# A retention layer and a squared-ReLU FFN on one core: additions moved from GpSimd to VectorE, outer sums made in phase one, inner products interleaved

## The chip, the cores and the metric

The kernel runs on one core of a Trainium2 chip. The metric is device time in microseconds (us), the median of several runs. The profile is one execution of the program taken by the hardware profiler; TensorE, VectorE, ScalarE, GpSimd and SyncE stand in it as PE, DVE, ACT, POOL and SP, and PEld is TensorE's weight load.

## The reference

Inputs are float32 except `w_in` and `w_out`, which arrive as 64-bit floats and are rounded to float32 in the kernel.

```python
# q, k, v: (8, 8, 576, 64)
scores = scale * np.matmul(q, k.transpose(0, 1, 3, 2))
Dmat = np.where(rel >= 0, gamma[:, None, None] ** rel[None, :, :], 0.0)
attn_out = np.matmul(scores * Dmat[None, :, :, :], v)
x = attn_out.transpose(0, 2, 1, 3).reshape(4608, 512)
h = np.maximum(x @ w_in, 0.0)          # w_in: 512 x 2048
out = h * h @ w_out                    # w_out: 2048 x 512
```

## The kernel before

**Phase one** walks over 40 chunks of attention (five to each of eight batches: four of 128 tokens, one of 64). A chunk i goes through `turn` (transposes of q and k), `scores` and `retain`, one stage to an iteration, and its result lands transposed in `xT`. When 512 tokens are there they make a block (nine in all), and the block's first FFN product is cut into 28 steps, four groups (`mp`) of seven, which `ffn` deals out between the attention's stages by tokens. The schedule is manual: each engine takes its instructions in the order in which the code records them.

Both FFN products are made with Strassen's scheme in Winograd's form, seven products instead of eight (`PRODUCTS`). The left operands are the four quarters A11, A12, A21, A22 and sums S1 to S4, the right ones B quarters and T1 to T4. Products add up in three PSUM tiles a, b and c, so a product that adds to a tile waits until the copy of what the tile held so far has been taken. In phase one a product is `h_a`, `h_b` or `h_c`: four float32 matmuls of 256 columns, each of which TensorE runs as two passes. `ffn_in` takes the results out of PSUM, adds them, squares them and leaves the quarters g11, g12, g21, g22 of the FFN's hidden layer in SBUF; `keep_g` stores the four of a group in DRAM (`g_dram`).

**Weights.** `w_in` comes in 16 pieces and `w_out` in 16, each rounded by `round_a` and `round_b`: integer work on VectorE, three passes on ScalarE, two multiplications on GpSimd. `sum_w_in` makes the four weight sums of a piece pair on GpSimd. `prepare` does one piece at a time, every second step of block 0 and later every seventh step; the `w_out` pieces and their sums go to `w2_dram`.

**Phase two** makes the second FFN product, block by block, with Strassen twice: seven outer products `ffn_out(n, j)`, each of seven inner products of four float32 matmuls of 128 columns (`o_a`, `o_b`, `o_c`, eight passes each; 63 times 7 = 441 inner products in all). The outer sums S1 to S4 of a block's quarters are made here by `outer_sum` over 128x2048 elements (S1 and S3 on GpSimd, S2 and S4 on VectorE), the inner sums of the next outer product by `inner_sums` over 128x512 (two on VectorE, two on GpSimd) after the fourth inner product. An outer product's inner products run in the order `INNER`, and its results p1, u2, p15 and r are 128x128 additions. At its end one or two 128x512 additions put r into the output quarters c11 to c22.

SyncE issues all loads and stores on one queue, in the order of the code.

Of the kernel before, what the change touches and what calls it, by code (L numbers as in the profile page):

```python
# [36 lines left out]
INNER = (1, 0, 2, 4, 3, 5, 6)  # L37
# [3 lines left out]
def kernel(  # L41
# [10 lines left out]
):  # L52

# [57 lines left out]
    g_dram = dram.tile([N_BLK, 4, 128, N_M, HT], F32, name="g_dram")  # L111
    room = [const.tile([128, N_M * HT], F32, name=f"room{j}") for j in range(7)]
# [68 lines left out]
    def round_a(j):  # L181
        lo, hi, frac, sign = words_of(j)
        exp = exp_of(j).bitcast(U32)
        t = piece_dst(j).bitcast(U32)
        nc.vector.tensor_scalar(exp, hi, 20, 0x7FF, op0=ALU.logical_shift_right, op1=ALU.bitwise_and)

        nc.vector.tensor_scalar(t, as_dst(j, hi), 0xFFFFF, 0x100000, op0=ALU.bitwise_and, op1=ALU.bitwise_or)

        nc.scalar.activation(frac, lo, AF.Copy, scale=2.0 ** -52)

        nc.scalar.activation(exp, exp, AF.Relu, bias=exp_bias[:, 0:1], scale=2.0 ** 23)

        nc.scalar.activation(sign, hi, AF.Sign, bias=exp_bias[:, 1:2], scale=-1.0)

    def round_b(j):
        lo, hi, frac, sign = words_of(j)
        t = piece_dst(j)
        nc.gpsimd.tensor_tensor(exp_of(j), exp_of(j), sign, op=ALU.mult)
        nc.vector.scalar_tensor_tensor(t, t.bitcast(U32), 2.0 ** -20, as_dst(j, frac), op0=ALU.mult, op1=ALU.add)  # L199
        nc.gpsimd.tensor_tensor(t, t, as_dst(j, exp_of(j)), op=ALU.mult)  # L200

    def sum_w_in(m):

        a11, a12, a21, a22, s1, s2, s4 = (w_in[m // 2][:, m % 2, j, :, :] for j in range(NP))
        nc.gpsimd.tensor_tensor(s1, a21, a22, op=ALU.add)
        nc.gpsimd.tensor_tensor(s2, s1, a11, op=ALU.subtract)
        nc.gpsimd.tensor_tensor(s4, a12, s2, op=ALU.subtract)
        nc.gpsimd.tensor_tensor(a21, a11, a21, op=ALU.subtract)

    def sum_w_out(m):  # L210

        mh = m // N_MQ
        b11, b12, b21, b22 = (stage[0][:, j, 2 * mh:2 * mh + 2, :] for j in range(4))
        t1, t2, t4 = (stage[1][:, j, 2 * mh:2 * mh + 2, :] for j in range(3))
        nc.vector.tensor_tensor(t1, b12, b11, op=ALU.subtract)
        nc.vector.tensor_tensor(b12, b22, b12, op=ALU.subtract)
        nc.vector.tensor_tensor(t2, b22, t1, op=ALU.subtract)
        nc.vector.tensor_tensor(t4, b21, t2, op=ALU.subtract)

    def keep_w_out(mq):  # L220

        for st_, at in ((stage[0], slice(0, 4)), (stage[1], slice(4, 7))):
            b11, b12, b21, b22, t1, t2, t4 = (st_[:, :, j, :] for j in range(NP))
            nc.vector.tensor_tensor(t1, b12, b11, op=ALU.subtract)
            nc.vector.tensor_tensor(b12, b22, b12, op=ALU.subtract)
            nc.vector.tensor_tensor(t2, b22, t1, op=ALU.subtract)
            nc.vector.tensor_tensor(t4, b21, t2, op=ALU.subtract)
            nc.sync.dma_start(w2_dram[at, :, mq, :].rearrange("o p f -> p o f"),
                              st_.rearrange("p o s f -> p o (s f)"))

    n_made = [0]

    def prepare():

        j = n_made[0]
        if j > len(pieces):
            return
        n_made[0] += 1

        for part in ((finish, begin) if j > N_W1 else (begin, finish)):  # L240
            part(j if part is begin else j - 1)
# [458 lines left out]
```

## Time and profile before

| | |
|---|---|
| median of 3 runs | 1276.17 us (1274.11 to 1276.55) |
| the profiled execution | 1276.56 us, its span 1274.9 us |
| TensorE busy, matmuls | 1087.6 us, 85% of the span |
| VectorE busy | 750.3 us, 59% |
| GpSimd busy | 467.3 us, 37% |
| ScalarE busy | 204.0 us, 16% |

The span runs from the first instruction to the last. Matmuls are pipelined and their ends are modelled, so a busy TensorE is not one at its full pace; how fast it goes is read from the distance between the starts of its groups. Clock 1.0 in a row means 2.4 GHz granted, 0.5 means 1.2 GHz.

### The profile page before, as it was taken

The numbers are of one execution on the slowest core, as the hardware profiler recorded it, in microseconds if no ns is written. First come the engines' busy times: TensorE is split into PE (matmuls) and PEld (weight loads), VectorE is DVE, ScalarE is ACT, GpSimd is POOL, SyncE is SP. The second block draws the span as 40 slices with busy tenths as digits, with TensorE's granted clock in tenths as the row PEclk, the third lists the DMA queues.
The fourth block names the chain that finished last, engine by engine and source line by source line (L and its number), as shares of the span: only waits on it lengthen the run. The fifth ranks groups of instructions, "written<-read, shape, count | busy, mean of one in ns | idle before, by whom it ended". The sixth has DMA issues, their size and how long they took to land. (4 is left out here: it accounts for less than half of the span.)

```text
span 1274.9 us, 19815 instructions
## 1 busy us (share of the span) xinstructions
PE 1087.6 (85%) x8168; PEld 981.9 (77%) x8168; DVE 750.3 (59%) x1108; ACT 204.0 (16%) x443; POOL 467.3 (37%) x346
## 2 busy tenths in 40 slices
PE   6389979989898999999999587787878788787788
PEld 5377868878687888887878487787877787787788
DVE  4588656656566444444444475757566656666755
ACT  4344212232231121111100000000000000000000
POOL 3888312323132121212110544434434444353532
PEclk9689989989899999999999797989889888888889
DMA  9834754664653644442177343131303030303000
GB/s 243 223 89 123 180 196 116 162 208 133 192 131 127 159 125 112 104 105 69 67 308 259 130 169 103 63 125 41 132 35 132 34 132 34 132 34 133 34 34 34
DMA packets 158362, 158.20 MB, mean 124 GB/s; under 512 B 114880, under 2 KB 124096, under 8 KB 152768
## 3 DMA queue, kind: packets, MB, share of 16 engines
q1 hardware_dynamic: 158272, 156.93, 40.8%
q8 instruction: 65, 1.06, 0.4%
q14 instruction: 25, 0.20, 0.1%
HBM read 96.88 MB, written 60.03 MB: 123 GB/s over the span
## 5 line engine op out<-in xcount | busy, mean ns | idle before, releaser
L406 PE MATMUL h_b<-room,w 128*128 128x256 f32 x864 | 223.9, 405 | 55.5 <-DVE room L425 33.6
L576 PE MATMUL o_b<-w,room 128*128 128x128 f32 x1176 | 172.9, 298 | 99.9 <-DVE small L581 99.9
L576 PEld LDWEIGHTS o_b<-w,room 128*128 128x128 f32 x1176 | 156.0, 209 | 107.5 <-issue 63.3
L406 PEld LDWEIGHTS h_b<-room,w 128*128 128x128 f32 x864 | 168.5, 201 | 85.8 <-DVE room L425 35.8
L576 PE MATMUL o_c<-w,room 128*128 128x128 f32 x1008 | 144.1, 290 | 0.0
L406 PE MATMUL h_a<-room,w 128*128 128x256 f32 x576 | 140.5, 388 | 0.0
L406 PE MATMUL h_c<-room,w 128*128 128x256 f32 x576 | 138.4, 383 | 0.0
L576 PEld LDWEIGHTS o_c<-w,room 128*128 128x128 f32 x1008 | 134.9, 208 | 0.0
L406 PEld LDWEIGHTS h_a<-room,w 128*128 128x128 f32 x576 | 109.9, 194 | 16.9
L423 POOL TENSOR_TENSOR room<-room 128x512 f32<-128x512 f32 x36 | 39.1, 1085 | 225.8 <-ACT room L422 220.6
L406 PEld LDWEIGHTS h_c<-room,w 128*128 128x128 f32 x576 | 107.4, 191 | 14.6
L326 POOL TENSOR_TENSOR vs<-v_ld,dv 128x512 f32<-128x512 f32 (+1 forms) x40 | 43.1, 1077 | 132.0 <-issue 61.2
L413 DVE SCALAR_TENSOR_TENSOR room<-room 128x512 f32<-128x512 f32 x108 | 86.8, 804 | 3.7
L418 DVE TENSOR_TENSOR room<-h_b,room 128x512 f32<-128x512 f32 x36 | 24.9, 692 | 108.3 <-PE h_b L406 108.0
L547 POOL TENSOR_TENSOR room<-a,room 128x512 f32<-128x512 f32 x24 | 30.6, 1273 | 127.3 <-PE o_c L576 50.8
L200 POOL TENSOR_TENSOR w<-w,w 128x512 f32<-128x512 f32 x32 | 42.0, 1314 | 84.1 <-DVE w L199 68.3
L425 DVE TENSOR_TENSOR room<-h_b,room 128x512 f32<-128x512 f32 x36 | 24.8, 689 | 72.5 <-PE h_b L406 72.5
L547 POOL TENSOR_TENSOR room<-room,room 128x512 f32<-128x512 f32 x21 | 26.6, 1268 | 100.5 <-PE o_c L576 65.4
L344 PE MATMUL x_ps<-ret,vs 128*64 128x128 f32 (+1 forms) x640 | 59.3, 276 | 4.2 <-POOL vs L326 4.2
L322 DVE TENSOR_TENSOR ret<-sc,msk 128x512 f32<-128x512 f32 (+1 forms) x80 | 47.1, 629 | 22.2 <-PE sc L317 22.2
L587 ACT COPY r<-o_a 128x128 f32<-128x128 f32 x54 | 14.3, 265 | 267.1 <-PE o_a L576 154.4
L576 PE MATMUL o_a<-w,a 128*128 128x128 f32 x384 | 55.5, 292 | 0.0
(101 smaller groups left out, 1739.6 us busy)
## 6 DMA issues: line engine op xcount, KB each, us to landing
g_dram<-room SPq DMA_DIRECT2D x36, 1024.0 KB, 4.9
a<-g_dram SPq DMA_DIRECT2D x24, 1024.0 KB, 5.5
w<-w_dram SPq DMA_DIRECT2D x7, 1792.0 KB, 9.0
room<-g_dram SPq DMA_DIRECT2D x12, 1024.0 KB, 5.6
out_dram<-room SPq DMA_DIRECT2D x18, 512.0 KB, 3.4
q_ld<-in_q_dram SPq DMA_DIRECT2D x32, 256.0 KB, 5.0
k_ld<-in_k_dram SPq DMA_DIRECT2D x32, 256.0 KB, 5.1
v_ld<-in_v_dram SPq DMA_DIRECT2D x32, 256.0 KB, 5.2
```

The lines of the kernel that those rows point to most:

```text
L200: nc.gpsimd.tensor_tensor(t, t, as_dst(j, exp_of(j)), op=ALU.mult)
L322: nc.vector.tensor_tensor(r[:cs, :, :cs], sc[e][:cs, :, :cs], msk[:cs, :, :cs].to_broadcast([cs, HP, cs]), op=ALU.mult)
L326: nc.gpsimd.tensor_tensor(vs[:cs], loaded[i][2][:cs], dv[:cs, :, ci:ci + 1].to_broadcast([cs, H, D]), op=ALU.mult)
L344: nc.tensor.matmul(p[half, hp, :cs], lhsT=s["vs"][:cs, 2 * hp + e, :], rhs=s["ret"][e][:cs, hp, :cs], start=(ci == 0 and hp == 0), stop=Tr ...
L406: nc.tensor.matmul(p[:, mm, :], lhsT=w[:, c, :], rhs=xs[n][right][:, c, :], start=(j in OPENS and mm == 0 and c == 0), stop=(j in CLOSES a ...
L413: nc.vector.scalar_tensor_tensor(t, t, 0.0, t, op0=ALU.max, op1=ALU.mult)
L418: nc.vector.tensor_tensor(u2, p, p1, op=ALU.add)
L423: nc.gpsimd.tensor_tensor(g11, g11, g11, op=ALU.mult)
L425: nc.vector.tensor_tensor(g22, p, p15, op=ALU.add)
L547: nc.gpsimd.tensor_tensor(s4, x12, s2, op=ALU.subtract)
L576: nc.tensor.matmul(p, lhsT=lhs[il][:, m, :], rhs=w_out[j][:, m, WO_SLOT[ir], :], start=(i in OPENS and m == 0), stop=(i in CLOSES and m == ...
L587: nc.scalar.copy(r11, p)
```

## The change

- In phase two the outer sums are gone. They are made in phase one instead, by `g_sums`, four 128x512 additions on VectorE for each group of a block, and `g_dram` keeps seven operands instead of four; phase two then reads one stored operand for each outer product k = 0 to 62 (`fetch_g(k)`, four outer products ahead).
- The four inner sums are all on VectorE (`inner_sums`), and the inner products of two neighbouring outer products alternate: in step k the products 0, 1, 2, 3 of k stand between the products 4, 5, 6 of k - 1.
- `sum_x`, `sum_w_in` and the second multiplication of a weight piece move from GpSimd to VectorE. GpSimd keeps one multiplication of a piece, the decay of v (`vs`) and the square of g11.
- Block 0 is made plainly: 16 steps `first_in`, each four float32 matmuls of 512 columns. `prepare` does one piece in each step, and a step of block 0 counts as two of the 28 in the dealing-out.
- The work on `w_out` is cut into 123 parts (`w_out_parts`), one behind each of the first four steps of a group from block 1 on; what is left is done at the start of the last block.
- The buffers of phase one become one tile `room`, cut by hand. Phase two uses parts of it again: the output tile `o_room` lies where the last group's operands lay.

The core of the diff:

```diff
-INNER = (1, 0, 2, 4, 3, 5, 6)
...
-    g_dram = dram.tile([N_BLK, 4, 128, N_M, HT], F32, name="g_dram")
-    room = [const.tile([128, N_M * HT], F32, name=f"room{j}") for j in range(7)]
+    g_dram = dram.tile([N_BLK, NP, 128, N_M, HT], F32, name="g_dram")
+
+    room = const.tile([128, 15872], F32, name="room")
...
-        nc.gpsimd.tensor_tensor(t, t, as_dst(j, exp_of(j)), op=ALU.mult)
...
+        def four():
+            nc.vector.tensor_tensor(t, t, as_dst(j, exp_of(j)), op=ALU.mult)
...
+    def sum_w_in(mp):
+
+        a11, a12, a21, a22, s1, s2, s4 = (w_in[mp][:, :, j, :, :].rearrange("p m c f -> p m (c f)") for j in range(NP))
+        nc.vector.tensor_tensor(s1, a21, a22, op=ALU.add)
...
+    def w_out_parts():
...
+            one, two, three, four = round_parts(j)
+            yield from (one, two, three)
...
-        nc.gpsimd.tensor_tensor(b12, b22, b12, op=ALU.subtract)
-        nc.gpsimd.tensor_tensor(t4, b21, t2, op=ALU.subtract)
+        nc.vector.tensor_tensor(b12, b22, b12, op=ALU.subtract)
+        nc.vector.tensor_tensor(t4, b21, t2, op=ALU.subtract)
...
+    def g_sums(n, mp):
+
+        g = g_of(mp)
+        return [
+            lambda: nc.vector.tensor_tensor(g["S1"], g["S3"], g["A22"], op=ALU.add),
+            lambda: nc.vector.tensor_tensor(g["S2"], g["S1"], g["A11"], op=ALU.subtract),
+            lambda: nc.vector.tensor_tensor(g["S3"], g["A11"], g["S3"], op=ALU.subtract),
+            lambda: nc.vector.tensor_tensor(g["S4"], g["A12"], g["S2"], op=ALU.subtract),
+            lambda: nc.sync.dma_start(g_dram[n, :, :, 2 * mp:2 * mp + 2, :].rearrange("s p m t -> p s (m t)"),
+                                      g_room[mp % 2].rearrange("p s m t -> p s (m t)")),
+        ]
...
+    def first_in(j):
...
+        for c in range(N_DM):
+            nc.tensor.matmul(p.rearrange("p h t -> p (h t)"), lhsT=w[:, c, :], rhs=xT[0][:, c, :],
+                             start=(c == 0), stop=(c == N_DM - 1))
...
+        if j in (6, 0, 1, 2, 3):
+            some()
+        if j < 4:
+            for f in w_out_steps:
+                f and f()
+                break
...
+            owed[0] -= 2 if steps[0][0] == 0 else 1
...
+    A_room = [late.tile([128, N_M * HT], F32, name=f"a{j}") for j in range(4)] + [part(8192), part(10240)]
+    s_room = [part(13824), part(0), part(2048)]
+    o_room = [part(at).rearrange("p (h j d) -> p h j d", h=2, j=2) for at in (4096, 6144)]
...
-            "S1": (nc.gpsimd, "A21", "A22", ALU.add),
-            "S2": (nc.vector, "S1", "A11", ALU.subtract),
-            "S3": (nc.gpsimd, "A11", "A21", ALU.subtract),
-            "S4": (nc.vector, "A12", "S2", ALU.subtract),
...
-        nc.gpsimd.tensor_tensor(s3, x11, x21, op=ALU.subtract)
-        nc.gpsimd.tensor_tensor(s4, x12, s2, op=ALU.subtract)
...
+    for k in range(N_K + 1):
+        sums_next = inner_sums(k + 1)
+        if k < N_K:
+            inner(k, 0)
+        for e in range(3):
+            if k > 0:
+                inner(k - 1, 4 + e)
+            if e == 2 and k > 0:
+                outer(k - 1)
+            if k < N_K:
+                inner(k, 1 + e)
+            if sums_next[e]:
+                sums_next[e]()
+        if sums_next[3]:
+            sums_next[3]()
+        fetch_g(k + 4)
```

Where the instructions stand now, at three places. **VectorE in phase two, before:** one outer product, the one ahead of whose successor a 128x2048 sum stands (L581, L583: u2 and p15; L585, L589, L591: r; L544, L545: inner sums; L596: an output quarter; L533: an outer sum).

```order
L581 TENSOR_TENSOR small<-o_b,small 128x128
L583 TENSOR_TENSOR small<-o_c,small 128x128
L585 TENSOR_TENSOR r<-o_b,small 128x128
L544 TENSOR_TENSOR room_97<-room_101 128x512
L545 TENSOR_TENSOR room_97<-room_97,room_101 128x512
L589 TENSOR_TENSOR r<-o_c,small 128x128
L591 TENSOR_TENSOR r<-o_b,small 128x128
L596 TENSOR_TENSOR room_95<-r,room_95 128x2x256
L533 TENSOR_TENSOR s_4345<-a_4344,s_4345 128x2048
```

VectorE in phase two now, one step k (L630, L632, L634: r of k - 1; L624, L626: u2 and p15 of k; L588 to L591: the four inner sums of k + 1; L645: an output quarter).

```order
L630 TENSOR_TENSOR r<-o_b,small 128x128
L624 TENSOR_TENSOR small<-o_b,small 128x128
L588 TENSOR_TENSOR room<-room 128x512
L632 TENSOR_TENSOR r<-o_c,small 128x128
L626 TENSOR_TENSOR small<-o_c,small 128x128
L589 TENSOR_TENSOR room<-room 128x512
L634 TENSOR_TENSOR r<-o_b,small 128x128
L645 TENSOR_TENSOR room<-r,room 128x2x256
L590 TENSOR_TENSOR room<-room 128x512
L591 TENSOR_TENSOR room<-room 128x512
```

The 128x2048 sum has gone, and the other two inner sums of each step have come from GpSimd; the results of k - 1 and of k alternate.

**TensorE in phase two, before:** the end of one outer product and the beginning of the next; each row is four float32 matmuls, `w_91` and `w_92` are the weights of the two.

```order
L576 MATMUL o_b<-w_91,s_4345 128x128 x4
L576 MATMUL o_b<-w_92,room_98 128x128 x4
L576 MATMUL o_a<-w_92,room_101 128x128 x4
L576 MATMUL o_c<-w_92,room_98 128x128 x4
L576 MATMUL o_b<-w_92,room_98 128x128 x4
```

TensorE in phase two now, from product 0 of one outer product (`w_92`) on, between the last three of the one ahead (`w_91`).

```order
L617 MATMUL o_a<-w_92,a_4404 128x128 x4
L617 MATMUL o_b<-w_91,room 128x128 x4
L617 MATMUL o_b<-w_92,room 128x128 x4
L617 MATMUL o_c<-w_91,room 128x128 x4
L617 MATMUL o_c<-w_92,room 128x128 x4
L617 MATMUL o_b<-w_91,a_4403 128x128 x4
L617 MATMUL o_a<-w_92,a_4404 128x128 x4
```

Before, two products stood between the first two into tile b with the same weights; now five do, and three between the second and the third.

**VectorE in phase one, before:** the end of one group and the beginning of the next, with a weight piece (L418, L420, L432: results taken from PSUM; L413: a square; L199: rounding; L215: a weight sum; L304: attention).

```order
L432 TENSOR_TENSOR room_95<-h_b,room_97 128x512
L413 SCALAR_TENSOR_TENSOR room_95<-room_95 128x512
L418 TENSOR_TENSOR room_98<-h_b,room_98 128x512
L304 TENSOR_TENSOR qT<-qT_ps,dq 128x512
L420 TENSOR_TENSOR room_98<-h_c,room_98 128x512
L199 SCALAR_TENSOR_TENSOR w_91<-w_91,w_90 128x2x256
L215 TENSOR_TENSOR w_92<-w_91 128x256
```

VectorE in phase one now, the beginning of one group (L411 to L413: the group before's outer sums; L468, L470, L475: results taken from PSUM; L196, L202, L209, L212: parts of `w_out` pieces; L338: attention).

```order
L202 TENSOR_SCALAR w_91<-w_90 128x2x256
L468 TENSOR_TENSOR room<-h_b,room 128x512
L411 TENSOR_TENSOR room<-room 128x512
L209 SCALAR_TENSOR_TENSOR w_91<-w_91,w_90 128x2x256
L470 TENSOR_TENSOR room<-h_c,room 128x512
L412 TENSOR_TENSOR room<-room 128x512
L212 TENSOR_TENSOR w_91<-w_91,w_90 128x2x256
L338 TENSOR_TENSOR ret_1225<-sc_1215,msk 128x512
L338 TENSOR_TENSOR ret_1227<-sc_1216,msk 128x512
L413 TENSOR_TENSOR room<-room 128x512
L196 TENSOR_SCALAR w_92<-w_90 128x512
L475 TENSOR_TENSOR room<-h_b,room 128x512
```

Four outer sums (the first stands ahead of this piece) and up to four weight parts now stand among the results of a group; before, only the results stood there, and now and then a whole weight piece.

## Rows read from the trace of the kernel before

**Rows 1.** Six stages of the span: busy us (instructions) by engine, granted clock, DMA.
```profile
0.00:41.60 41.60, 26.70 (x296) 23.08 (x296) 18.24 (x27) 16.96 (x30) 18.73 (x27) 0.88 1.06 245
41.60:138.50 96.90, 74.08 (x494) 61.32 (x492) 72.39 (x94) 40.92 (x69) 77.33 (x68) 0.88 0.54 144
138.50:446.00 307.50, 282.03 (x2066) 238.05 (x2066) 181.25 (x291) 72.79 (x137) 84.13 (x71) 0.96 0.56 158
446.00:584.00 138.00, 137.12 (x1055) 116.92 (x1056) 63.19 (x96) 23.61 (x49) 23.32 (x21) 1.00 0.44 109
584.00:723.00 139.00, 120.74 (x744) 103.23 (x739) 60.70 (x82) 16.28 (x33) 26.29 (x19) 0.93 0.47 172
723.00:1275.00 552.00, 446.94 (x3529) 439.29 (x3528) 354.57 (x522) 33.42 (x126) 237.54 (x142) 0.90 0.24 84
```

**Rows 2.** Two of these stages, instructions of L406 alone (phase one's products): PE, PEld.
```profile
41.60:138.50 96.90, 56.78 (x224) 44.42 (x224) 0.88 0.54 144
446.00:584.00 138.00, 103.14 (x449) 82.98 (x448) 1.00 0.44 109
```

**Rows 3.** Timeline of TensorE at the end of phase one: start, us, instruction.
```profile
702.08 1.89 PE L406 MATMUL h_b<-room,w 128*128 128x256 f32 x8
703.81 1.89 PE L406 MATMUL h_c<-room,w 128*128 128x256 f32 x8
```

**Rows 4.** Timeline of TensorE in phase two, where it runs without a wait.
```profile
942.79 1.06 PE L576 MATMUL o_a<-w,a 128*128 128x128 f32 x8
943.69 1.06 PE L576 MATMUL o_c<-w,room 128*128 128x128 f32 x8
944.58 1.06 PE L576 MATMUL o_b<-w,a 128*128 128x128 f32 x8
```

**Rows 5.** Timeline at one block boundary of phase two; idle time in brackets.
```profile
895.11 4.51 POOL L533 TENSOR_TENSOR a<-a,a 128x2048 f32<-128x2048 f32 x1
...
896.47 3.70 DVE L605 TENSOR_TENSOR room<-r,room 128x512 f32<-128x512 f32 x1
...
900.09 3.35 DVE L533 TENSOR_TENSOR s<-room,a 128x2048 f32<-128x2048 f32 x1
...
903.79 1.62 PE L576 MATMUL o_b<-w,room 128*128 128x128 f32 x6 [5.07 <-DVE small L581]
```

**Rows 6.** Waits of TensorE, whole span: total us, times, longest.
```profile
PE o_b L576 <- DVE small L581: 99.9, 27, 5.9
PE h_b L406 <- DVE room L425: 33.6, 6, 13.9
...
PE x_ps L344 <- POOL vs L326: 4.2, 1, 4.2
```

**Rows 7.** Groups by shape, whole span: busy us, mean ns | idle before.
```profile
L602 DVE TENSOR_TENSOR room<-r,room 128x512 f32<-128x512 f32 x9 | 42.1, 4681 | 0.9
...
L423 POOL TENSOR_TENSOR room<-room 128x512 f32<-128x512 f32 x36 | 39.1, 1085 | 225.8 <-ACT room L422 220.6 <-DMA v_ld<-in_v_dram 5.2
...
L418 DVE TENSOR_TENSOR room<-h_b,room 128x512 f32<-128x512 f32 x36 | 24.9, 692 | 108.3 <-PE h_b L406 108.0 <-ACT room L416 0.2
...
L581 DVE TENSOR_TENSOR small<-o_b,small 128x128 f32<-128x128 f32 x63 | 18.0, 286 | 28.4 <-ACT small L580 28.4
...
L544 DVE TENSOR_TENSOR room<-a 128x512 f32<-128x512 f32 x24 | 16.3, 681 | 0.0
...
L598 DVE TENSOR_TENSOR room<-r,room 128x512 f32<-128x512 f32 x9 | 12.6, 1403 | 0.9
...
L607 DVE TENSOR_TENSOR room<-r,room 128x512 f32<-128x512 f32 x9 | 6.8, 758 | 0.9
```

**Rows 8.** All engines in the last block of phase one, as in rows 1.
```profile
650.00:705.00 55.00, 52.63 (x237) 45.76 (x236) 24.53 (x34) 5.02 (x9) 6.68 (x6) 0.97 0.87 315
```

**Rows 9.** DMA issues: KB each, median us from issue to landing.
```profile
g_dram<-room SPq DMA_DIRECT2D x36, 1024.0 KB, 4.9
...
out_dram<-room SPq DMA_DIRECT2D x18, 512.0 KB, 3.4
```

More of the change, by code (lines that the diff above doesn't have):

```diff
@@ L210, in sum_w_out @@
[L210 to L229, printed above, removed]
+        t = piece_dst(j)
@@ L267 @@
+        if j > 0:
+            for f in parts.pop(j - 1)[2:]:
+                f and f()
+            if j + 8 < N_W1:
+                fetch_w(j + 8)
     dq = only.tile([128, HP, S], F32, name="dq")
@@ L292 @@
     u_ps = [None]
-    xT = {n: room[5 + n % 2].rearrange("p (c t) -> p c t", c=N_DM) for n in range(N_BLK)}
+    xT = {n: xT_room[n % 2] for n in range(N_BLK)}
     def turn(i):
@@ L512, with part @@
-    s2_room = late.tile([128, N_M * HT], F32, name="s2")
-    s_room = [room[2], room[3]]
-    o_room = [room[j].rearrange("p (h j d) -> p h j d", h=2, j=2) for j in range(2)]
-    def fetch_g(n, name):
-        if n < N_BLK:
-            nc.sync.dma_start(A(n, name), g_dram[n, A_NAMES.index(name), :, :, :])
+    def part(at):
+        return room[:, at:at + N_M * HT]
+    A_room = [late.tile([128, N_M * HT], F32, name=f"a{j}") for j in range(4)] + [part(8192), part(10240)]
+    s_room = [part(13824), part(0), part(2048)]
@@ L609, in store @@
-    def store(n, half):
-        row = n * TOK + half * HT
-        nc.sync.dma_start(out[row:row + HT, :].rearrange("(a p) d -> p a d", p=128), o_room[n % 2][:, half, :, :])
-    for name in A_NAMES[:3]:
-        fetch_g(0, name)
-    while steps:
-        n, mp, j = steps[0]
-        if n == N_BLK - 1 and mp == 0 and j == 0:
-            assert n_made[0] == len(pieces) + 1
-            for e in range(3):
-                fetch_w2(e)
-        if n == N_BLK - 1 and j == 1 and mp:
-            fetch_w2(2 + mp)
-        step()
-        if n == N_BLK - 1 and mp == N_MP - 1 and j == 2:
-            fetch_g(0, "A22")
-            outer_sum(0, "S1")
-            outer_sum(0, "S2")
-            inner_sums(0, 0)
-            outer_sum(0, "S3")
@@ L653 @@
-    store(N_BLK - 1, 1)
+        for to, with_ in {1: [(c21, c11)], 2: [(c12, c21)], 3: [(c11, c11)], 4: [(c22, c12), (c21, c21)],
+                          5: [(c12, c12)], 6: [(c21, c21)]}.get(j, []):
+            nc.vector.tensor_tensor(to, r, with_, op=ALU.add)
+        if j >= 5:
+            half = j - 5
+            row = n * TOK + half * HT
+            nc.sync.dma_start(out[row:row + HT, :].rearrange("(a p) d -> p a d", p=128), o[:, half, :, :])
+    for j in range(3):
+        fetch_g(j)
@@ new lines @@
+    n_last = 0
+    while steps:
+        n, f, *args = steps[0]
+        if n == N_BLK - 1:
+            if n_last == 0:
+                for f in w_out_steps:
+                    f and f()
+                for j in range(3):
+                    fetch_w2(j)
+            elif n_last % NP == 1 and n_last > NP:
+                fetch_w2(2 + n_last // NP)
+            if n_last == N_MP * NP - 5:
+                for f in inner_sums(0):
+                    f()
+            n_last += 1
+        step()
```

322 lines of the change are left out of this document (156 added, 166 removed).

## The prediction

> **What bounds the kernel now.** I read the stages first [rows 1]. From 446 to 584 us the kernel runs as it should: TensorE is busy for 137.1 of 138.0 us at clock 1.00. The other stages are not like that. Block 0's stage takes 96.9 us for the 224 passes that the other stages need too [rows 2], and there GpSimd is busy for 77.3 us and VectorE for 72.4. Phase two takes 552 us, with TensorE busy for 447 and a clock of 0.90. So I asked what TensorE's own pace would make of each stage.
>
> In phase one a product (eight passes of 256 columns) starts 1.73 us after the one ahead of it [rows 3], 48.4 us for a block's 28. In phase two an inner product (eight passes of 128) takes 1.79/2 = 0.895 us [rows 4], 395 us for all 441. Phase two loses 157 us against that. The waits say to whom: in 27 of them TensorE stood for 99.9 us behind the small addition L581 [rows 6]. One of them read back [rows 5]: GpSimd makes an outer sum for 4.51 us; beside it the 128x512 addition L605 lasts 3.70 us; only then comes VectorE's own outer sum, 3.35 us; L581 stands behind that, and TensorE has been idle for 5.07 us. After each such idle time TensorE runs at half clock for a while, which is the 0.90.
>
> **Attention's share.** Two blocks in the undisturbed 138.0 us are 96.9 us of products; the other 41.1 us are attention for 1024 tokens, 0.040 us a token.
>
> **Phase two (outer sums gone, inner sums on VectorE, interleaving).** In a step VectorE has four inner sums at 0.68 us (L544), five small additions at 0.29 (L581) and on average one output addition at 0.76 (L607), all from [rows 7]: 2.72 + 1.43 + 0.76 = 4.9 us beside TensorE's seven products, 6.27 us. VectorE is loaded to 78%, and TensorE is the bound if nothing is late. The tightest pair is product 4 and product 6 of an outer product, both into tile b: between them stand three products, 2.7 us, in which VectorE must take r22. When r22's product ends, VectorE can at worst be busy with the sums of the step before: laid end to end from the start of a step, its queue (r22 from 1.8 us, u2 from 2.7, a sum, r12, p15, a sum, r21 from 5.4, one output addition, two sums) runs to 7.8 us, or 8.5 where j is 4 and there are two output additions; the next r22 is due at 8.0. So it is late by 0.5 us of 2.7 in one step of seven, and no wait comes of it. The inner sums of k + 1 are needed from 8.0 us on for S2, and S2 stands ready at 5.5. Operands are read four steps, 25 us, ahead. Sum: 63 x 6.27 = 395 us.
>
> At the seam to phase two two things are not covered. VectorE still has the last group's addition, square and three sums, 4.2 us, before u2. And the output tile lies where the last group's operands lay, so the first r11 and r22 wait for that group's store: four slots land in 4.9 us [rows 9], seven in an estimated 7 to 8, issued 4 us after the last product; TensorE has some 8 us of products to go on with. I take 4.5 us. At the end stand r21, an output addition and the store: 0.3 + 0.8 + 3.4 [rows 9] = 4.5 us. Phase two: 395 + 4.5 + 4.5 = 404 us. From below it can't be under 395; from above, rival B.
>
> **Start and block 0.** The first product of block 0 starts at 41.6 us now; TensorE waits there once, 4.2 us, for `vs`, which stands behind weight sums in GpSimd's queue [rows 6], so 37.5. A plain step has eight passes of 512 columns, which no row shows. From 112 ns (128) and 216 ns (256 columns) a pass of 512 lies between 424 and 432 ns; I take the upper, 3.46 us a step and 55.3 for 16. That is 6.9 more than 28 products; the gain is that nothing waits for weight sums. A step counts double, so 585 tokens of attention go between, 23.5 us. VectorE has the pieces' second multiplication and the sums of weights and of g instead of GpSimd: about eight pieces at 2.2 us, 16 pairs of 128x256 squares at 0.84, and 2 x 0.68 us a step of sums, near 4.4 us a step while pieces last, over TensorE's 3.46 plus 1.5 of attention's share in part of them. I allow 5 us for waits. Block 0 ends at 37.5 + 55.3 + 23.5 + 5 = 121 us, against 138.5. Bounds: 116 with no wait, 130 with VectorE behind in every one of its first ten steps.
>
> **Blocks 1 to 8.** Products 8 x 48.4 = 387; attention for the other 3511 tokens 141 us. VectorE now: 63.2/2 = 31.6 us a block [rows 1], plus 16 outer sums at 0.68 (10.9), two additions of `sum_x` (1.4) and a seventh of the `w_out` work (my sum from its shapes: 69 us, 9.8), together 53.7 of 68.9 us. In the mean it keeps up. In a group without attention (12.1 us) I walked its queue: r of product 4 (L475) can begin when its product ends, and is done 1.0 us before product 6 needs it; a GpSimd square (1.085 us, L423) that holds up a sum there eats that. For waits of this kind I allow 8 us over eight blocks. The last block begins with what is left of `w_out`, eleven parts or 5.8 us of VectorE, ahead of `sum_x` of which product 1 needs two additions: 7 us. Its stores, 1792 KB instead of 1024, run beside the loads of weights; now 315 GB/s flow there [rows 8], and a store must have landed some 10 us after issue, before its buffer is written again: 3 us. Now VectorE's stall L425 costs 13.9 us at once there [rows 6], behind outer sums that wait for a load; that one is gone. Sum: 387 + 141 + 8 + 7 + 3 = 546; phase one ends at 667.
>
> **Sum.** 121 + 546 + 404 = 1071 us of span; the profiled execution lies 1.7 us over its span (1276.56 and 1274.9) and 0.4 over the median: **1073 us**.
>
> **Rivals.** *A, VectorE and GpSimd still shut each other out.* L605 above and L602 (mean 4.681 us, where its twin L607 takes 0.758 [rows 7]) show an addition from SBUF standing still while GpSimd works; L418, which reads PSUM, stays at 0.692. GpSimd keeps 11.7 us a block in the undisturbed stage [rows 1] and gets some multiplications of weights more. If each of the 28 groups with weight work loses the 1.1 us of a square to it, that is 31 us and some 4 at half clock: 1108 us. Against it: attention between the products gives VectorE room in most groups. The Trainium skill, SBUF — State Buffer, section Who interferes with whom, makes it a lock: VectorE's second read port is GpSimd's, and an instruction with two SBUF inputs and a GpSimd one that reads SBUF exclude each other for a whole instruction. By that rule, the trace agrees (3.70 us beside a sum of 4.51), and the change leaves GpSimd's squares beside more such additions than before.
>
> *B, evictions late in phase two.* With VectorE at 78% in strict order, a late r22 or u2 may cost each step a microsecond: 63 us, 1136. For it: L581 is where the waits are now. Against it: today's waits are longer than any row without a GpSimd sum explains.
>
> *C, DMA around the seam.* The last block has to move some 23 MB (six weight tiles, three operands, four stores, the last of `w2_dram`); at 315 GB/s [rows 8] that is 73 us for its 53, 20 us late: 1093.
>
> *D, slower than now.* If additions between SBUF tiles stay as long as they are now beside GpSimd, VectorE is the bound everywhere. With d us for each, a block's VectorE time is 47 d + 22 and a step's 5 d + 1.4, and 121 + 8 x (47 d + 22) + 63 x (5 d + 1.4) + 9 reaches 1275 at d = 1.27. L598 averages 1.403, which gives 1365. Against it: L544 at 0.681 in phase two, with GpSimd's sums around it.
>
> **Chances.** My forecast 0.55 (1050 to 1090: nothing at the allowances below, twice them above), A 0.2, C 0.1, B 0.08, D 0.03, better than 1045 0.04 (pauses before block 1 vanish as well). The range goes from 1042 to 1125: it holds forecast, A and C, 0.85, and leaves out B and D. About 0.2% is what a measurement of this kernel can tell from no change; faster by more 0.96, same 0.01, slower 0.03.
>
> **What would show it.** Phase two: products 0.895 us apart from first to last, clock near 1.00, no wait of TensorE for a VectorE addition over 0.5 us, VectorE at some 78%. Seam: one stop of a few us behind the store. Block 0: ends near 121 us, VectorE busier than GpSimd. Blocks 1 to 8: VectorE at some 80%; one stop of 7 us at the last block's first products. Wrong it would be if TensorE waited often for L475's result or `sum_x`'s, each time with a GpSimd row beside it (A), or if stores took over 10 us outside the last block (C).

## The result, and the profile after

The changed kernel takes 1092.87 us (median of 4 runs, 1088.82 to 1093.79) beside 1275.81 for the kernel before: a ratio of 0.856, 95% interval [0.854, 0.859]. The forecast was 1073 us, the range 1042 to 1125. The profiled execution took 1092.35 us, its span 1090.6. The missing 20 us can be placed to a stage by TensorE's own rows: from the span's start to block 0's first product, from there to block 1's, to phase two's first, and to the end.

| us | start | block 0 | blocks 1 to 8 | phase two |
|---|---|---|---|---|
| kernel before | 41.6 | 99.7 | 581.8 | 551.7 |
| predicted | 37.5 | 83.5 | 546 | 404 |
| measured | 41.3 | 100.5 | 544.3 | 404.5 |

Two terms hold, two don't. The prediction set its 121 us for the end of block 0 against 138.5, which is where block 0's last product ended before; block 1's first product started at 141.3 there and starts at 141.8 now, so start and block 0 together have gained nothing. The same stages as windows, the answer to [rows 1] (the columns are those of that group; the second row shown is two blocks without a long stop, the third the last block):

```profile
41.30:141.80 100.50, 83.52 (x460) 44.95 (x456) 72.03 (x120) 39.12 (x85) 21.93 (x18) 0.88 0.53 145
...
349.60:486.50 136.90, 136.03 (x1034) 115.78 (x1034) 105.53 (x165) 32.62 (x63) 26.87 (x22) 1.00 0.66 191
621.10:686.20 65.10, 53.20 (x226) 45.20 (x226) 43.13 (x66) 4.74 (x8) 4.16 (x4) 0.92 0.91 347
686.20:1090.60 404.40, 396.36 (x3529) 395.74 (x3527) 281.99 (x633) 33.43 (x126) 0.00 (x0) 0.99 0.53 192
```

Phase two is full: TensorE busy for 396.4 of 404.4 us at clock 0.99, GpSimd without an instruction. In the two blocks VectorE is busy for 105.5 us, 52.8 a block, where 53.7 was worked out. Block 0 still has the clock of 0.88 that it had before [rows 1]. The waits of TensorE over the whole span say where the rest is (total, times, longest), the answer to [rows 6]:

```profile
PE h_b L456 <- DVE room L396: 11.3, 5, 6.8
PE kT_ps L317 <- DVE ret L338: 11.0, 3, 6.1
PE x_ps L360 <- POOL vs L342: 6.0, 2, 3.4
PE qT_ps L317 <- DMA q_ld<-in_q_dram: 5.9, 2, 4.2
PE h_b L456 <- DVE room L475: 5.1, 2, 5.0
PE qT_ps L317 <- ACT room L368: 3.5, 1, 3.5
PE o_b L617 <- DVE room L630: 3.0, 1, 3.0
PE sc L333 <- DVE qT L320: 2.5, 1, 2.5
```

The 99.9 us behind L581 have no successor: L624, which makes u2 now, isn't among the waits, and of the other small additions only L630 (r) appears, once, at the seam. `ret`, L368 and `qT` (L320), which TensorE waits for here, are attention's own steps in block 0. Groups by shape (busy us, mean ns, idle before) answer to [rows 7]:

```profile
L645 DVE TENSOR_TENSOR room<-r,room 128x512 f32<-128x512 f32 x63 | 42.8, 691 | 1.9
L588 DVE TENSOR_TENSOR room<-a 128x512 f32<-128x512 f32 x43 | 29.3, 682 | 0.7 <-DMA a<-g_dram 0.7
```

The output addition, which averaged 4681 ns in one of its forms before, now takes 691 in all 63. Phase two's timeline (start, duration) answers to [rows 4]: six inner products between the first row and the last, 925.74 to 931.10, are 5.36 us, 0.893 each.

```profile
925.74 1.95 PE L617 MATMUL o_a<-w,a 128*128 128x128 f32 x16
...
931.10 1.06 PE L617 MATMUL o_b<-w,a 128*128 128x128 f32 x8
```

The seam, answer to [rows 5]: the last group's store is issued at 690.45, and TensorE stops for 3.01 us until it has landed and L630 may write.

```profile
690.45 0.37 SPq L414 DMA_DIRECT2D g_dram<-room  x1
...
697.65 0.29 DVE L630 TENSOR_TENSOR room<-o_b,small 128x128 f32<-128x128 f32 x1 [4.46 <-DMA g_dram<-room]
...
697.99 1.16 PE L617 MATMUL o_b<-w,a 128*128 128x128 f32 x8 [3.01 <-DVE room L630]
```

And block 0 around its longest stop. The scores that the mask L338 (`ret`) reads are done at 59.57, and the mask starts at 69.58. In between VectorE works through two weight pieces and the squares L439 of two products; the second pair of squares stands behind ScalarE's Relu L438, which stands behind its rounding pass L205. TensorE stands for 6.11 us, since the PSUM buffer of the next transposes is free only after the mask.

```profile
57.55 2.02 PE L333 MATMUL sc<-qT,kT 64*128 64x128 f32 x16 [2.47 <-DVE qT L320]
...
59.86 1.52 DVE L202 TENSOR_SCALAR w<-w 128x512 uint32<-128x512 uint32 x1
...
62.69 1.85 DVE L439 TENSOR_TENSOR room<-room 128x256 f32<-128x256 f32 x2
...
66.08 0.74 ACT L205 ACTIVATE w<-w,exp_bias 128x512 f32<-128x512 uint32 x1
66.72 0.64 ACT L438 ACTIVATE room<-h_ps 128x256 f32<-128x256 f32 x2
66.90 1.28 POOL L206 TENSOR_TENSOR w<-w 128x512 f32<-128x512 f32 x1 [2.98 <-ACT w L205]
67.12 2.53 DVE L439 TENSOR_TENSOR room<-room 128x256 f32<-128x256 f32 x2 [0.52 <-ACT room L438]
...
69.58 1.27 DVE L338 TENSOR_TENSOR ret<-sc,msk 128x512 f32<-128x512 f32 x2
...
70.31 1.11 PE L317 MATMUL kT_ps<-ident,k_ld 128*128 128x128 f32 x4 [6.11 <-DVE ret L338]
...
107.67 0.76 DVE L439 TENSOR_TENSOR room<-room 128x256 f32<-128x256 f32 x2
```

The last row is a pair of squares with no GpSimd row beside it: 0.76 us. The two pairs ahead of the mask took 1.85 and 2.53 beside GpSimd's L206 and L342, and the integer pass L202 1.52 beside L206 where it takes 0.41 elsewhere. So some 3.8 of the 10 us ahead of the mask are VectorE rows made longer beside GpSimd (0.42 us a square alone). In all of block 0, 10 of the 32 squares ran beside a GpSimd row, 1.31 us on average; the other 22 took 0.42.

### The profile page after: what moved, and what is told of

It is laid out like the page before. It is cut to its first block, busy times and chain, and to the rows that moved or that the text cites. A ratio compares the mean times of both kernels' runs of the same rounds, so it can differ in the third digit from the quotient of the medians.

```text
span 1090.6 us, 19392 instructions
## 1 busy us (share of the span) xinstructions
PE 1034.1 (95%) x8072; PEld 912.9 (84%) x8072; DVE 780.7 (72%) x1422; ACT 207.4 (19%) x467; POOL 130.3 (12%) x116
## 5 line engine op out<-in xcount | busy, mean ns | idle before, releaser
L456 PE MATMUL h_b<-room,w 128*128 128x256 f32 x768 | 190.2, 391 | 16.4 <-DVE room L396 11.3
L456 PEld LDWEIGHTS h_b<-room,w 128*128 128x128 f32 x768 | 144.7, 193 | 40.3 <-issue 9.5
L617 PE MATMUL o_b<-w,room 128*128 128x128 f32 x1168 | 144.9, 276 | 0.2 <-DVE room L589 0.2
L617 PEld LDWEIGHTS o_b<-w,room 128*128 128x128 f32 x1168 | 137.7, 193 | 0.5 <-DVE room L589 0.4
L617 PE MATMUL o_c<-w,room 128*128 128x128 f32 x1008 | 123.0, 275 | 0.0
L617 PE MATMUL o_a<-w,a 128*128 128x128 f32 x688 | 87.0, 278 | 0.0
L617 PEld LDWEIGHTS o_a<-w,a 128*128 128x128 f32 x688 | 82.5, 194 | 0.1
L463 DVE SCALAR_TENSOR_TENSOR room<-room 128x512 f32<-128x512 f32 x96 | 67.8, 706 | 3.3
L468 DVE TENSOR_TENSOR room<-h_b,room 128x512 f32<-128x512 f32 x32 | 22.1, 691 | 59.8 <-PE h_b L456 57.4
L342 POOL TENSOR_TENSOR vs<-v_ld,dv 128x512 f32<-128x512 f32 (+1 forms) x40 | 46.5, 1161 | 131.0 <-issue 89.4
L433 PE MATMUL h_ps<-room,w 128*128 128x512 f32 x128 | 61.9, 633 | 0.0
L338 DVE TENSOR_TENSOR ret<-sc,msk 128x512 f32<-128x512 f32 (+1 forms) x80 | 46.9, 627 | 16.7 <-PE sc L333 16.7
L475 DVE TENSOR_TENSOR room<-h_b,room 128x512 f32<-128x512 f32 x32 | 22.0, 687 | 43.8 <-PE h_b L456 36.4
L356 PE MATMUL x_ps<-qT,u_sb 128*64 128x128 f32 (+1 forms) x512 | 51.0, 278 | 0.0
```

Of the source, the lines that this page charges most:

```text
L338: nc.vector.tensor_tensor(r[:cs, :, :cs], sc[e][:cs, :, :cs], msk[:cs, :, :cs].to_broadcast([cs, HP, cs]), op=ALU.mult)
L342: nc.gpsimd.tensor_tensor(vs[:cs], loaded[i][2][:cs], dv[:cs, :, ci:ci + 1].to_broadcast([cs, H, D]), op=ALU.mult)
L356: nc.tensor.matmul(p[half, hp, :cs], lhsT=u_sb[ci % 2][:, hp, half], rhs=s["qT"][:, hp, :cs], start=(hp == 0), stop=False, skip_group_chec ...
L433: nc.tensor.matmul(p.rearrange("p h t -> p (h t)"), lhsT=w[:, c, :], rhs=xT[0][:, c, :], start=(c == 0), stop=(c == N_DM - 1))
L456: nc.tensor.matmul(p[:, mm, :], lhsT=w[:, c, :], rhs=xs[n][right][:, c, :], start=(j in OPENS and mm == 0 and c == 0), stop=(j in CLOSES a ...
L463: nc.vector.scalar_tensor_tensor(t, t, 0.0, t, op0=ALU.max, op1=ALU.mult)
```

## The experiments

Unless another kernel is named, each is the changed kernel with one edit. The table has the median, the ratio to the kernel before and the four stages of the profiled execution, found as above.

| kernel | us | ratio, 95% interval | start | block 0 | 1 to 8 | phase two |
|---|---|---|---|---|---|---|
| changed kernel | 1092.87 | 0.856 [0.854, 0.859] | 41.3 | 100.5 | 544.3 | 404.5 |
| before, all additions on VectorE | 1183.47 | 0.929 [0.922, 0.936] | 39.7 | 100.2 | 574.5 | 467.0 |
| not interleaved | 1094.26 | 0.859 [0.853, 0.865] | 40.9 | 100.2 | 544.6 | 407.8 |
| two inner sums on GpSimd | 1089.97 | 0.856 [0.849, 0.862] | 42.7 | 98.5 | 544.5 | 403.3 |
| two outer sums on GpSimd | 1097.81 | 0.862 [0.856, 0.868] | 41.9 | 100.6 | 551.1 | 402.9 |
| block 0: product first | 1087.21 | 0.852 [0.850, 0.855] | 41.0 | 97.0 | 544.7 | 404.4 |
| block 0: seven pieces not loaded | 1091.24 | 0.855 [0.854, 0.857] | 42.3 | 98.4 | 544.7 | 404.4 |
| block 0: Strassen | 1089.51 | 0.854 [0.852, 0.856] | 41.0 | 102.8 | 541.1 | 402.9 |
| block 0: pieces on GpSimd | 1104.52 | 0.867 [0.865, 0.868] | 44.9 | 112.4 | 540.8 | 402.8 |
| block 0: no VectorE work on pieces | 1075.00 | 0.843 [0.842, 0.845] | 41.0 | 86.5 | 542.0 | 402.8 |
| parts in five steps | 1081.23 | 0.847 [0.846, 0.848] | 42.0 | 98.6 | 534.4 | 404.5 |
| three repairs | 1072.78 | 0.842 [0.841, 0.844] | 41.9 | 96.7 | 527.8 | 404.3 |
| and squares on ScalarE | 1060.54 | 0.831 [0.830, 0.833] | 42.4 | 87.7 | 526.2 | 404.7 |

Kernels with the same code in a stage differ there by up to 2 us in block 0 (98.5 to 100.5), 4 in blocks 1 to 8 (540.8 to 544.7) and 2 in phase two (402.8 to 404.5). A difference of that size is not read as an effect below.

### What the gain is made of

**All additions on VectorE, nothing else.** The kernel before, with every addition that the change moves put on VectorE at its old place, outer sums and order included.

```diff
-        nc.gpsimd.tensor_tensor(s3, x11, x21, op=ALU.subtract)
+        nc.vector.tensor_tensor(s3, x11, x21, op=ALU.subtract)
...
-            "S1": (nc.gpsimd, "A21", "A22", ALU.add),
+            "S1": (nc.vector, "A21", "A22", ALU.add),
```

> The kernel before with one part of the change alone: every addition that the change takes off GpSimd is on VectorE, nothing is interleaved, the outer sums stay in phase two. If the exclusion of VectorE by GpSimd was the main cost of phase two: 60 to 100 us faster than before, 1180 to 1215 us. If the chain at a block's seam (two outer sums one after the other, 4.5 + 3.35 us, then 2 x 2.3 on one engine) was: 20 to 50 us faster.

Phase two falls from 551.7 us to 467.0, although VectorE now does all the work of both, and 1183 us lies in the first of the two ranges expected. The output addition L602, 4681 ns before [rows 7], takes 692. That row, and the waits of TensorE that are left:

```profile
L602 DVE TENSOR_TENSOR room<-r,room 128x512 f32<-128x512 f32 x9 | 6.2, 692 | 0.9
...
PE o_b L576 <- DVE small L581: 51.1, 25, 3.4
PE h_b L406 <- DVE room L425: 30.8, 4, 13.8
```

L581 still comes late 25 times, but the longest stop is 3.4 us instead of 5.9 [rows 6]: what is gone is GpSimd's sum ahead of VectorE's, since GpSimd has no instruction left in that phase two. Blocks 1 to 8 gain 7 us here, 37 in the changed kernel. The stops behind L425 stay in this run (30.8 us, 33.6 before), and L475, which has its place in the changed kernel, has 5.1. Which part of the change removed them no run shows.

**Not interleaved.** The seven inner products of an outer product in a row, its sums between them.

```diff
-        for e in range(3):
-            if k > 0:
-                inner(k - 1, 4 + e)
-            ...
+        for i in range(NP):
+            inner(k, i)
+            if i in (1, 2, 4, 5) and sums_next[(1, 2, 4, 5).index(i)]:
+                sums_next[(1, 2, 4, 5).index(i)]()
+        outer(k)
```

> Phase two without interleaving: the seven inner products of one outer product stand one after another in the order 0 to 6, all inner sums on VectorE, stored outer sums. If it is the interleaving that hides the additions: in each of 63 outer products TensorE waits for r22 ahead of product 6 (one product, 0.9 us, between) and now and then for u2; 0.5 to 1.5 us each, 30 to 95 us in all, 1120 to 1185 us. If the outer sums and GpSimd were what cost phase two its time and interleaving only trims it: under 15 us slower than the changed kernel.

3.3 us of phase two, and a time whose interval overlaps that of the changed kernel. 2.9 of the 3.3 us stand at the seam, where the stop behind the store is 5.4 us instead of 3.0 and one of 0.7 takes the place of one of 0.2:

```profile
PE o_b L617 <- DVE room L630: 5.4, 1, 5.4
...
PE o_b L617 <- DVE small L624: 0.7, 1, 0.7
```

After that TensorE waits for no addition. So my theory that the five products in between hide the additions falls, with all of them on VectorE. Of phase two's 147 us, taken away in this order, 85 come from the engine alone (551.7 to 467.0), 59 from the rest of the change in that phase (to 407.8, this run: outer sums made in phase one, stored operands, another order of the products and the sums spread between them, not tried apart), 3 from interleaving.

**Two inner sums on GpSimd again.**

```diff
-            lambda: nc.vector.tensor_tensor(x["S3"], x["A11"], x["A21"], op=ALU.subtract),
-            lambda: nc.vector.tensor_tensor(x["S4"], x["A12"], x["S2"], op=ALU.subtract),
+            lambda: nc.gpsimd.tensor_tensor(x["S3"], x["A11"], x["A21"], op=ALU.subtract),
+            lambda: nc.gpsimd.tensor_tensor(x["S4"], x["A12"], x["S2"], op=ALU.subtract),
```

> Two of the four inner sums of phase two go back to GpSimd, everything else of the change stays, the interleaving too. If GpSimd's lock on VectorE's additions is what made phase two wait: VectorE's two sums and output additions (0.68 us) grow beside it to 1.2 us and more, but a step has 1.4 us of room, so at most 10 us slower. If interleaving alone covers it: within 3 us of the changed kernel.

No cost in time, though the two engines plainly hinder each other: the output addition goes from 691 ns to 1607 beside GpSimd's sums of 1651.

```profile
L645 DVE TENSOR_TENSOR room<-r,room 128x512 f32<-128x512 f32 x63 | 100.5, 1607 | 1.9
L590 POOL TENSOR_TENSOR room<-a 128x512 f32<-128x512 f32 x43 | 71.0, 1651 | 11.4 <-DMA g_dram<-room 6.8 <-DMA a<-g_dram 4.5
```

VectorE, busy for 266 of 403 us in this run, has the room for it, and nothing stands behind L645 that is needed soon. Whether interleaving is what covers the longer rows here isn't shown: two sums on GpSimd without interleaving was not run.

**Two outer sums on GpSimd**, S1 and S3 of `g_sums`.

```diff
-            lambda: nc.vector.tensor_tensor(g["S1"], g["S3"], g["A22"], op=ALU.add),
+            lambda: nc.gpsimd.tensor_tensor(g["S1"], g["S3"], g["A22"], op=ALU.add),
...
-            lambda: nc.vector.tensor_tensor(g["S3"], g["A11"], g["S3"], op=ALU.subtract),
+            lambda: nc.gpsimd.tensor_tensor(g["S3"], g["A11"], g["S3"], op=ALU.subtract),
```

> In phase one two of the four outer sums of a group (S1 and S3) are made on GpSimd, 72 additions. Rival A (they shut each other out): VectorE's other SBUF additions and squares grow, GpSimd's square of g11 comes later, TensorE waits for L475; 5 to 30 us slower. If VectorE's load is the limit in phase one: faster, by up to 10 us.

Blocks 1 to 8 get 6.8 us longer, the kernel 4.9 (the intervals overlap), at the edge of the 5 to 30 that I expected. The square L463 on VectorE takes 792 ns instead of 706, the sums on GpSimd 1467. TensorE's wait for L475 doesn't grow (4.3 us, 5.1 in the changed kernel), though I had expected that; the one for `sum_x` (L396) does, from 11.3 to 16.7, and in block 0 the one for `ret` from 11.0 to 14.3. So rival A's mechanism is there, and it costs where VectorE's results are awaited; in blocks 1 to 8 the changed kernel pays little for it, since only 5 of the 96 squares L463 run beside a GpSimd row there.

```profile
L463 DVE SCALAR_TENSOR_TENSOR room<-room 128x512 f32<-128x512 f32 x96 | 76.0, 792 | 3.3
L412 POOL TENSOR_TENSOR room<-room 128x512 f32<-128x512 f32 x36 | 52.8, 1467 | 1.8
```

### Where the missing 20 us are

At first two theories stood for block 0: the order within a step (the weight piece is recorded ahead of the product and its results), or the transfers (the DMA engines are busy for 0.98 of the time up to 41.3 us and stay so until 64, beside other loads that attention waits for).

**Product first.**

```diff
-        prepare()
-        f(*args)
+        if n == 0:
+            f(*args)
+            prepare()
+        else:
+            prepare()
+            f(*args)
```

> In block 0 a step's products and the taking of its results are recorded ahead of the next weight piece, not behind it; nothing else changes. Theory 1 (VectorE and ScalarE work through a weight piece of 2.2 us each before they take the step's results, and TensorE's attention stands behind that): the stage from the first product of block 0 to the first of block 1, 100.5 us in the changed kernel, falls by 8 to 14 us, and the waits of TensorE for the masked scores (11.0 us) and for the scaled q (2.5 us) mostly go. Theory 2 (the pieces come late from DRAM, because the DMA engines are full until 60 us): the stage changes by under 3 us.

Block 0 is 1.5 to 3.5 us shorter than where its code is unchanged, under half of what I expected. TensorE's wait for `qT` is gone (it is in some runs with unchanged code too), that for L368 is 4.4 us, and the waits for `ret` stay at 10.9.

**Seven pieces not loaded.** The last seven pieces of `w_in` are worked on without being fetched.

```diff
-            if j + 8 < N_W1:
+            if False:
                 fetch_w(j + 8)
```

> The last seven of the sixteen w_in pieces are not loaded, so block 0 and all later blocks work with wrong weights there; every instruction on the engines stays. Theory 2: VectorE's wait for a piece (3.7 and 1.4 us) and what follows it go, the stage of block 0 falls from 100.5 us by 6 to 12 us. Theory 1: by under 4 us, since the queue behind the pieces is as long.

98.4 us is what unchanged code can give, and the waits for `ret` are the same 11.0 us: not the transfers of the pieces.

**Block 0 by Strassen**, in 28 steps, with weight sums on VectorE (the core of the edit).

```diff
-            return [(0, first_in, j) for j in range(N_W1)]
...
-            owed[0] -= 2 if steps[0][0] == 0 else 1
+            owed[0] -= 1
```

> Block 0 goes back to Strassen's 28 steps with a weight piece in every second one; all else of the change stays. If plain products are what makes block 0 quicker than it was (100.5 us for 585 tokens of attention, 96.9 us for 512 before): the kernel is slower than the changed one by 5 to 20 us. If they only cost 6.9 us of TensorE and the engines' moves did the rest: 0 to 7 us faster. Theory 1 leans to the second, since half as many pieces fall on a step.

Block 0 and blocks 1 to 8 together take 643.9 us instead of 644.8. The plain block is neither gain nor loss, so its 6.9 us of more products aren't the missing time either. Its stops are others. With Strassen one of 14.3 us in block 0 is for `sum_x` (L398 here), which the plain block doesn't need; 15.5 us stood there in the kernel before.

```profile
PE h_b L460 <- DVE room L398: 24.5, 6, 14.3
```

Both theories explain little, and a third was left, V: VectorE's queue itself. The masks stand in it behind whatever is done for a piece, wherever in the step that is. Two runs try it from opposite sides.

**Pieces on GpSimd.** `w_in`'s second multiplication and the weight sums go back to GpSimd.

```diff
-            nc.vector.tensor_tensor(t, t, as_dst(j, exp_of(j)), op=ALU.mult)
+            (nc.gpsimd if j < N_W1 else nc.vector).tensor_tensor(t, t, as_dst(j, exp_of(j)), op=ALU.mult)
...
-        nc.vector.tensor_tensor(s1, a21, a22, op=ALU.add)
+        nc.gpsimd.tensor_tensor(s1, a21, a22, op=ALU.add)
```

> The changed kernel, except that the second multiplication of w_in's 16 pieces and the sums of sum_w_in are on GpSimd again (w_out's stay on VectorE). Theory V: block 0's stops come from VectorE's queue, in which the masks (ret) stand behind weight work; about 1.5 us a step leave that queue, so TensorE's wait for ret falls from 11 us to under 5 and block 0's stage from 100.5 us to 88 to 95. Theory A (VectorE and GpSimd shut each other out): the additions that stay on VectorE lengthen beside GpSimd's, ret comes no earlier, stage 100 us or more, 1092 us or more. Theory L (the loads of q, k and v at the start decide): stage and wait within 2 us of what they were.

Block 0 grows by 11.9 us and the wait for `ret` from 11.0 to 17.9, where theory V had expected under 5: taking instructions off VectorE made it later. The rows there say why (groups by shape, block 0's stage, the changed kernel's row first):

```profile
L439 DVE TENSOR_TENSOR room<-room 128x256 f32<-128x256 f32 x32 | 21.1, 698 | 22.4 <-ACT room L438 22.3
```

```profile
L439 DVE TENSOR_TENSOR room<-room 128x256 f32<-128x256 f32 x32 | 32.8, 1066 | 25.7 <-ACT room L438 25.7
L196 DVE TENSOR_SCALAR w<-w 128x512 uint32<-128x512 uint32 x11 | 6.5, 591 | 14.1 <-POOL w L212 14.1
...
L338 DVE TENSOR_TENSOR ret<-sc,msk 128x512 f32<-128x512 f32 x8 | 5.1, 678 | 0.0
```

The squares, with both inputs in SBUF, go from 698 to 1066 ns; the mask, which reads PSUM, stays at 678; and VectorE stands for 14.1 us behind GpSimd's multiplication. This is theory A of this run's expectation; how much of the 11.9 us comes from the longer rows and how much from the wait for GpSimd's multiplication is not shown. By the Trainium skill, SBUF — State Buffer, section Who interferes with whom, a GpSimd instruction that reads SBUF and a VectorE instruction with two SBUF inputs contend for a lock; these rows agree (1066 ns where 698 stood; the mask, not of that kind, 678).

**No VectorE work on pieces.** From the fourth piece on, VectorE's four instructions for a piece of `w_in` are left out (the core of the edit; ScalarE writes the low words as weights).

```diff
+        light = 3 <= j < N_W1
...
+            if light:
+                return
             nc.vector.scalar_tensor_tensor(t, t.bitcast(U32), 2.0 ** -20, as_dst(j, frac), op0=ALU.mult, op1=ALU.add)
...
+            if light:
+                return
             nc.vector.tensor_tensor(t, t, as_dst(j, exp_of(j)), op=ALU.mult)
```

> The changed kernel, except that from the fourth piece of w_in on VectorE does nothing for a piece: its shift, its mask, its two arithmetic passes are left out and ScalarE writes the low words straight into the weights, so that the weights are not those of the reference; ScalarE's three passes, GpSimd's multiplication, the loads and the weight sums stay. Theory V: the waits for ret go (11 us to under 2), TensorE is not thrown to half clock there, block 0's stage falls from 100.5 to 82 to 90 us. Theory L or ScalarE's queue: the waits stay in the same places under another name (L368, L320, q_ld) and the stage is 96 us or more.

Block 0 falls to 86.5 us with the same loads and as many ScalarE passes. Its waits, block 0 alone:

```profile
PE kT_ps L326 <- DVE ret L347: 4.6, 1, 4.6
PE qT_ps L326 <- ACT room L377: 1.5, 1, 1.5
```

So V holds; one stop for the mask is left, where I expected under 2 us. The run takes out more than places in the queue: ScalarE no longer waits for VectorE's integer passes, and 5 instead of 10 squares run beside a GpSimd row. The last run below leaves the pieces as they are.

**Parts in five steps.** The other big stop, 6.8 us at the start of the last block, was foreseen: eleven parts of `w_out` are left there.

```diff
-        if j < 4:
+        if j < 5:
             for f in w_out_steps:
```

> The parts of the w_out work stand behind five steps of a group instead of four, so that none is left at the start of the last block. The stop of 6.8 us there and its time at half clock go: 7 to 9 us faster than the changed kernel, 1084 us, if VectorE has room for it in the blocks ahead (it is busy for 77% there). If it has none (the lock with GpSimd eats it), waits for L475 appear there and the gain is under 3 us.

Blocks 1 to 8 lose 9.9 us, more than the stop itself; the wait for the late store (L475) falls too, from 5.1 to 3.1.

```profile
PE kT_ps L317 <- DVE ret L338: 11.0, 3, 6.1
PE h_b L456 <- DVE room L396: 5.8, 5, 1.9
```

**Three repairs.** Product first, five steps, and the first three weight reads of phase two spread over the last block.

```diff
-                for j in range(3):
-                    fetch_w2(j)
+                fetch_w2(0)
+            elif n_last in (4, 11):
+                fetch_w2(1 + n_last // 11)
```

> The changed kernel with three repairs: in block 0 a step's product stands ahead of the weight piece (alone -3.5 us of stage), the parts of w_out are dealt to five steps of a group (alone -10), and the reads of the first three weight tiles of phase two are issued over the last block (before its products 0, 4 and 11) instead of all at its start, so that the store of the group's operands isn't late (stop of 5 us). If the three are independent: 1092.9 - 3.5 - 11.6 - 3 = 1075, between 1071 and 1079. If the stop of the late store only moves to the first products of phase two: 1078 to 1081.

1072.8 us; blocks 1 to 8 lose 16.5. From the last blocks to the seam (waits, 600 to 720 us) nothing of size is left but the seam's stop, as in the changed kernel:

```profile
PE o_b L621 <- DVE room L634: 3.0, 1, 3.0
PE h_b L456 <- DVE room L396: 1.2, 1, 1.2
...
PE h_b L456 <- DVE room L475: 0.2, 1, 0.2
```

**And squares on ScalarE.** If the masks are late in VectorE's queue, something that can leave it without going to GpSimd should.

```diff
-            nc.vector.tensor_tensor(t, t, t, op=ALU.mult)
+            nc.scalar.activation(t, t, AF.Square)
```

> The version with the three repairs, and block 0's 32 squares on ScalarE, right behind its Relu, instead of VectorE (where they took 18.1 us in that stage, 0.60 each, and VectorE stood for 26 us behind the Relu ahead of them). Theory V: the masks (ret) come earlier, TensorE's wait for ret in block 0 falls from 10.5 us to under 5 and the stage from 96.7 us to 87 to 93; 1063 to 1069 us in all against 1072.8. Rival S: ScalarE's own queue takes VectorE's place (some 12 us more on its 40 of 97): the wait for ret moves to L368 and L322 by as much, the stage stays at 95 us or more, 1071 us or more.

1060.5 us, below the expected 1063 to 1069, and block 0 at 87.7. A square takes 0.42 us on ScalarE, also beside a GpSimd row. Waits of the whole span (some rows are left out):

```profile
PE qT_ps L317 <- ACT room L368: 5.5, 1, 5.5
...
PE h_b L456 <- DVE room L396: 4.1, 5, 1.2
...
PE kT_ps L317 <- DVE ret L338: 2.4, 1, 2.4
PE h_ps L433 <- ACT room L368: 1.1, 1, 1.1
```

The wait for `ret` falls by 8.1 us against the three repairs, that for L368 grows by 1.0 (5.6 to 6.6 in two stops), so rival S is small. VectorE's rows still lengthen in block 0 (6 of 10 L202 run beside a GpSimd row, 1.29 us each on average, 0.42 alone); with the squares gone from its queue the masks come early all the same. It is the fastest version here; it beats both kernels.

## Why the prediction was right, and what was mis-sized

**Phase two** (404, measured 404.5). Pace, seam and drain came as worked out: 0.893 us an inner product, one stop of 3.01 us and one of 0.24 at the seam. VectorE is at 70% and not 78: I had added up durations, but VectorE starts a row before the one ahead has ended (its durations in phase two add up to 308.7 us, in which it is busy for 282.0). What failed here is a reason, not a number: interleaving was to keep the additions off the path, and without it phase two is 3.3 us longer, nearly all of it at the seam. Rival B (63 us) was off by more still.

**Blocks 1 to 8** (546, measured 544.3). The flush of `w_out`'s parts stopped TensorE for 6.8 us (7 predicted), the late store for 5.0 (3 predicted). The 8 us allowed were for sums held up by a GpSimd square ahead of L475: that cost 0.1. The other waits for `sum_x` sum to 4.5, for which there was no term, so that the total came out is in part luck. The repairs gave 16.5 us with 10.5 us of stops less; against the shortest blocks 1 to 8 with the same code (540.8, pieces on GpSimd) it is 13.0 for 8.7. That fits the clock: around and after the two long stops of the last block the granted clock is 0.50 (1.2 GHz) from 627.7 to 634.5 and from 658.4 to 661.8 us, 0.92 over the block; with the three repairs the last block has 1.00. Rival C's place was right (347 GB/s, the store late), its 20 us weren't.

**The step that failed is block 0's allowance for waits**: 5 us, measured 21.7 (100.5 less 55.3 of products and 23.5 of attention). 17.0 of them are stops (`ret` 11.0, L368 3.5, `qT` 2.5). The other 4.7 fit the clock: it is 0.50 (1.2 GHz) from 57.7 to 74.7 and from 108.9 to 115.7 us, around the stops, and TensorE works for 12.7 us of that. I compared VectorE's sum with TensorE's, 4.4 us a step against 3.46 and up to 1.5, and took the small difference for the wait. But VectorE was at 72% there. What mattered was its order: a mask of 0.6 us waits for a piece's four instructions, for the squares, and through them for ScalarE's Relu behind its rounding passes. Two sizes in that sum were off as well: about twelve pieces fell in the stage, not eight, and a pair of squares took 1.40 us on average, not 0.84, because of the rows beside GpSimd. That what stands ahead of the masks is the cause is shown by two runs: without pieces on VectorE 86.5, with the squares elsewhere 87.7 (96.7 with them). In the latter the stops of block 0 (`ret` 2.4, L368 6.6) leave 78.7 us, which is the 78.8 of products and attention.

**The start** (37.5, measured 41.3) failed in the same way. Here the queue is GpSimd's. The weight sums left it and `vs` still came late, 6.0 us in two stops against 4.2 in one [rows 6], because it stands there behind a multiplication that waits for ScalarE's rounding:

```profile
24.77 1.38 POOL L206 TENSOR_TENSOR w<-w 128x512 f32<-128x512 f32 x1 [6.32 <-ACT w L205]
26.10 1.51 POOL L342 TENSOR_TENSOR vs<-v_ld,dv 128x512 f32<-128x512 f32 x1
```

For this no run was made; it is read from the trace alone.

**Rival A** (1108) lies 15 us from the measured time, the forecast 20, but A's loss isn't where it was placed: its 31 us were to come in the 28 groups with weight work, where the waits for L475 are 0.1 us without the late store. Its mechanism is in block 0, which its sum left out: rows made longer beside GpSimd are 3.8 of the 10 us ahead of the mask in the longest stop. No run parts this from the order; the last run, in which rows lengthen and the masks are early, suggests that they cost where a mask stands behind them. The rest of the sum, 100.5 - 83.5 = 17 and 41.3 - 37.5 = 3.8, less 1.7 in blocks 1 to 8, plus 0.5, is the 19.6 us by which the span passed 1071.

## What to carry to other kernels

An engine at 72% can still stop the one that waits for it: for each small instruction that releases the bottleneck, list what stands ahead of it in its queue and what those wait for, instead of comparing sums of busy time. Before moving work between VectorE and GpSimd, look at which rows lengthen side by side: here squares and additions with both inputs in SBUF did (0.42 to 1.31 us, 0.69 to 1.61), integer passes with one input too (0.41 to 1.52), a mask that reads PSUM did not (0.68); ScalarE took the same squares without that price (0.42). A stop costs its length and then some at the lower clock, so removing the few long ones (here eleven leftover parts and a bunch of early loads) repays more than their length: 16.5 us for 10.5.

## What the hardware showed that I had not expected

The price of VectorE and GpSimd side by side can be large in the rows and nothing in the time (L645 691 to 1607 ns, the time the same), or smaller in the rows and 12 us in the time (L439 698 to 1066 ns, with a wait for GpSimd's multiplication beside it), according to what stands behind. A float32 pass of 512 columns took 0.435 us (16 passes from 88.07 to 95.03 us of the changed kernel's block 0), just above the 0.432 that I took.
